# Attention and expert kernel on one core: in the last pair of heads, VectorE instead of GpSimd makes the second halves of the exponentials

## The chip, the cores and the metric

The kernel runs on one core of a Trainium2 chip. A core has five engines that work side by side, each through its own queue in order: TensorE (PE in the profile; PEld is its loading of weights), VectorE (DVE), ScalarE (ACT), GpSimd (POOL) and SyncE (SP), which here only starts transfers (DMA). They wait for one another through semaphores. The metric is the device time of one execution in microseconds (us), median of the runs.

## What is computed

Attention over clusters, and behind it a layer of eight experts of which each token uses two. Cut to what matters:

```python
# q, k, v: (4, 8, 768, 64); 16 centroids per head
mask = q_assign[:, :, :, None] == k_assign[:, :, None, :]
scores = np.where(mask, scale * np.matmul(q, k.transpose(0, 1, 3, 2)), -1e9)
scores = scores - np.max(scores, axis=-1, keepdims=True)
attn = np.exp(scores)
attn = attn / (np.sum(attn, axis=-1, keepdims=True) + 1e-09)
x = np.matmul(attn, v)            # then (3072, 512)
...
# top 2 of 8 experts per token, weights from a softmax of the two
h = np.maximum(x[mask] @ w1[e], 0.0)
out[mask] += top2_w[mask, k, None] * (h @ w2[e])
```

## The kernel before, in words

The 32 heads (4 batches of 8) are worked on as 16 pairs, `p` from 0 to 15. A pair has 12 steps: two heads `s`, and six blocks `kc` of 128 keys each. The loop of `attention` (L262 on) runs over steps `t`, 12 to a pair, and writes the instructions of all engines down in that order; a table `AT` of step numbers says at which step side work is put in. There is no other scheduler: each engine does its instructions in the order in which they are written.

One step of the main loop has three parts:

- `scores` (L477): TensorE makes the scores of 128 keys against 768 queries (four matmuls of 384 columns, L485), and ScalarE their exponentials in two instructions (L486) into a tile `pe` of 128x768 floats, six of which are in use in turn.
- `split_p` (L489), one step later: an exponential is used as the sum of two 16-bit numbers. The first half `hi` costs nothing: it is the upper 16 bits of the float, read in place as bfloat16 with every second element. The second half `lo`, a tile `pl` of 128x768 in float16 (five in turn), is the float minus `hi`, one subtraction (L495). In the kernel before, GpSimd makes all 192 of them.
- `values` (L498), four steps behind the scores: twelve matmuls with `hi` (L512, L514), then six with `lo` (L518), into an accumulator `av` that the two heads share. At the end of a head VectorE divides by the row sums (L523 to L526), and only then can the next head's values begin. At `kc` = 0 no values are made and at `kc` = 1 two rounds of them.

Between these, in the last two pairs (14 and 15), stands side work for the experts:

- GpSimd: the entries of the list of tokens of batch 2 (`g_list`, L697: a tiny memset as a spacer, L700, and an indirect DMA, L701), one per step up to step 183; and in steps 185 to 188 `gather_x` (L923): a tile `xg` is zeroed (L929) and rows of tokens are gathered into it by an indirect DMA (L930). The gathers need the list, which SyncE loads back when all its entries are written (L720).
- ScalarE and VectorE: the weights of the first expert are split into halves (`split_w1`, four pieces of 128x1024; L903 the copy on ScalarE, L904 the subtraction on VectorE).

After the last values come the experts (L731 on). The first instructions of TensorE there are transposes of three gathered tiles (L941), then the logits of the last batch, the gate, and the first expert's layers.

VectorE's largest part, the row maxima of pair p (L457), stands in the steps of the pair before it. In the last pair there is no next pair, and so no maxima.

Of the kernel before, what the change touches and what calls it, by code (L numbers as in the profile page):

```python
# [15 lines left out]
OP = mybir.AluOpType  # L16
# [27 lines left out]
class Kernel:  # L44
# [444 lines left out]
    def split_p(self, p, s, kc):  # L489

        nc, st = self.nc, self.st[p]
        pe = st["p", s, kc].rearrange("p a n -> p (a n)")
        hi = pe.bitcast(BF).rearrange("p (n two) -> p n two", two=2)[:, :, 1]
        lo = self.wk.tile([128, self.S], F16, name="pl", bufs=5)
        nc.gpsimd.tensor_tensor(lo, pe, hi, op=OP.subtract)  # L495
        st["p", s, kc] = hi, lo

    def values(self, p, s, kc):  # L498
# [553 lines left out]
```

## Time and profile before

| what | us |
|---|---|
| median of 3 runs | 1154.22 (1153.69 to 1156.89) |
| the profiled execution | 1154.92 |
| its span | 1153.1 |
| PE busy in the span | 1076.4 (93%) |
| DVE busy | 596.7 (52%) |
| ACT busy | 480.4 (42%) |
| POOL busy | 589.6 (51%) |
| the 192 splits of L495 on POOL | 280.6, 1471 ns each |

How to read it: the shares are means over a program of two halves. Attention takes the first 520 us or so, the experts the rest. Granted clock means the share of TensorE's full clock that it was given (1.00 is 2.4 GHz, 0.50 is 1.2 GHz). An engine that waits is shown with the instruction that released it. All times of the trace are from the start of the span.

### The profile page before, as it was taken

What the parts mean: (1) busy time and instruction counts of PE and PEld (TensorE: products, weight loads), DVE (VectorE), ACT (ScalarE), POOL (GpSimd) and SP (SyncE); (2) the same over time, 40 slices, a digit from 0 to 9 for tenths busy, and PEclk for the clock granted to TensorE, in tenths of its full rate; (3) what the DMA queues carried; (4) which work ended last, traced back from release to release, by engine and by line L of the source; (5) the groups of instructions that cost most, each with busy time, mean ns of one, the idle gap of its engine ahead of it and who ended that gap; (6) DMA issues with size and microseconds to landing.
All of it is one profiled execution on the core that took longest, in us unless ns stands there. A gap on an engine that the chain in (4) does not pass through costs nothing. (4 is left out here: it accounts for less than half of the span.)

```text
span 1153.1 us, 22350 instructions
## 1 busy us (share of the span) xinstructions
PE 1076.4 (93%) x8658; PEld 954.6 (83%) x8658; DVE 596.7 (52%) x1286; ACT 480.4 (42%) x961; POOL 589.6 (51%) x631
## 2 busy tenths in 40 slices
PE   4899899998999899869899999999999999999995
PEld 4588887898888788757799989889898898998984
DVE  5877665876687668436235334433344244433411
ACT  3475656675777566534133303223133132231300
POOL 4776664789578958991645224332343233423311
PEclk8899999999999999969999999999999999999998
DMA  8866776664656444113326225323352244323200
GB/s 224 189 151 152 188 185 194 158 158 110 192 122 159 113 127 122 33 43 118 109 75 210 81 102 166 120 93 109 127 172 73 77 162 129 118 83 131 74 31 31
DMA packets 87678, 144.46 MB, mean 125 GB/s; under 512 B 14296, under 2 KB 65880, under 8 KB 87057
## 3 DMA queue, kind: packets, MB, share of 16 engines
q1 hardware_dynamic: 72272, 106.45, 34.7%
q0 software_dynamic: 13712, 36.42, 9.4%
q8 instruction: 69, 1.13, 0.4%
q10 hardware_dynamic: 1584, 0.13, 0.1%
q14 instruction: 41, 0.33, 0.1%
HBM read 78.21 MB, written 26.53 MB: 91 GB/s over the span
## 5 line engine op out<-in xcount | busy, mean ns | idle before, releaser
L495 POOL TENSOR_TENSOR pl<-pe 128x768 f16<-128x768 f32 x192 | 280.6, 1471 | 97.4 <-ACT pe L486 90.0
L951 PE MATMUL ring<-xT,w1t 128*128 128x416 f32 (+2 forms) x1536 | 290.3, 350 | 0.0
L951 PEld LDWEIGHTS ring<-xT,w1t 128*128 128x128 f32 x1536 | 282.7, 188 | 6.6 <-DVE xT L904 0.3
L990 PE MATMUL ring<-w2t,hT 128*128 128x512 f32 x1152 | 273.7, 394 | 0.0
L990 PEld LDWEIGHTS ring<-w2t,hT 128*128 128x128 f32 x1152 | 214.5, 189 | 43.3
L486 ACT ACTIVATE pe<-ring,l 128x384 f32<-128x384 f32 x384 | 202.9, 578 | 102.5 <-PE ring L485 93.4
L1003 POOL DMA_INDIRECT out<-yo,lst x56 | 65.6, 1172 | 234.7 <-DVE yo L999 187.1
L457 DVE TENSOR_REDUCE aux<-ring 128x1 f32<-128x384 f32 x192 | 107.9, 562 | 94.6 <-PE ring L454 90.2
L485 PE MATMUL ring<-A 128*128 128x384 f32 x384 | 145.4, 379 | 0.0
L485 PE MATMUL ring<-B 128*128 128x384 f32 x384 | 134.3, 350 | 5.0 <-DMA B<-nt 4.9
L960 ACT ACTIVATE hT<-ring 128x416 fp32r<-128x416 f32 (+3 forms) x128 | 56.7, 488 | 180.6 <-PE ring L951 180.5
L961 DVE SCALAR_TENSOR_TENSOR hT<-ring,hT 128x416 fp32r<-128x416 f32 (+3 forms) x128 | 66.2, 553 | 124.0 <-ACT hT L960 123.8
L930 POOL DMA_INDIRECT xg<-xs,lst x56 | 65.5, 1170 | 124.9 <-PE ring L941 105.0
L454 PE MATMUL ring<-A 128*128 128x384 f32 x384 | 114.0, 372 | 14.5 <-DMA A<-mk 8.6
L999 DVE SCALAR_TENSOR_TENSOR yo<-ring,lst,xt 128x512 f32<-128x512 f32 (+1 forms) x49 | 36.7, 750 | 166.6 <-PE ring L990 146.1
L903 ACT ACTIVATE xT<-ring 128x512 fp32r<-128x512 f32 (+1 forms) x56 | 31.0, 565 | 178.0 <-PE ring L941 177.9
L457 DVE TENSOR_REDUCE mm<-ring 128x1 f32<-128x384 f32 x192 | 104.9, 546 | 0.0
L512 PE MATMUL av<-vv,pe 128*128 128x65 f16 x1152 | 100.9, 198 | 0.0
L514 PE MATMUL av<-vv,pe 128*128 128x64 f16 x1152 | 99.9, 196 | 0.0
L454 PEld LDWEIGHTS ring<-A 128*128 128x128 f32 x384 | 71.6, 197 | 31.0 <-ACT pe L486 14.1
L512 PEld LDWEIGHTS <-pe 128*128 128x128 bf16 x1152 | 83.6, 101 | 13.9 <-issue 11.4
L518 PE MATMUL av<-vv,pl 128*128 128x65 f16 x1152 | 68.9, 197 | 20.1 <-POOL spacer L700 12.6
(172 smaller groups left out, 1363.1 us busy)
## 6 DMA issues: line engine op xcount, KB each, us to landing
stg<-in_moe_w SPq DMA_DIRECT2D x64, 512.0 KB
A<-hl SPq DMA_DIRECT2D x30, 384.0 KB
B<-hl SPq DMA_DIRECT2D x30, 384.0 KB
vt<-in_v SPq DMA_DIRECT2D x8, 768.0 KB
out<-zt SPq DMA_DIRECT2D x12, 512.0 KB
xs<-xt SPq DMA_DIRECT2D x4, 1536.0 KB
A<-hl SPq DMA_DIRECT2D x60, 96.0 KB
B<-hl SPq DMA_DIRECT2D x30, 192.0 KB
```

The lines of the kernel that those rows point to most:

```text
L454: nc.tensor.matmul(t, A[:, 0, s, j * 128:j * 128 + 128], A[:, 1, s, n * 384:n * 384 + 384], start=True, stop=True)
L457: nc.vector.tensor_reduce(o, t, axis=X, op=OP.max, negate=True)
L485: nc.tensor.matmul(t, M[:, 1 - qi, s, ks], M[:, qi, s, ns], start=not qi, stop=bool(qi))
L486: nc.scalar.activation(pe[:, n], t, AF.Exp, bias=self.l64[:, 0:1], scale=self.scale)
L495: nc.gpsimd.tensor_tensor(lo, pe, hi, op=OP.subtract)
L512: nc.tensor.matmul(av[:, j, :], ph[:, js], vv[:, hh, kj, 64:129], start=(kc == 0 and j == 0), stop=False, skip_group_check=True)
L514: nc.tensor.matmul(av[:, j, :64], ph[:, js], vv[:, hh, kj, 0:64], start=False, stop=False, skip_group_check=True)
L518: nc.tensor.matmul(av[:, j, :], pl[:, js], vv[:, hh, kj, 64:129], start=False, stop=(kc == NJ - 1), skip_group_check=True)
L951: nc.tensor.matmul(p, self.w1t[:, wi, c, f * 128:f * 128 + 128], self.xT[:, xi, c, n0:n1], start=(i == 0), stop=(i == 3 * ND - 1))
L961: nc.vector.scalar_tensor_tensor(h1, x, 0.0, h0, op0=OP.max, op1=OP.subtract)
L990: nc.tensor.matmul(p, self.hT[:, hi, f, t * 128:t * 128 + 128], self.w2t[:, wi, f], start=(i == 0), stop=(i == 3 * NF - 1))
L1003: i = nc.gpsimd.indirect_dma_start(out=self.out, out_offset=bass.IndirectOffsetOnAxis(ap=en[:r, 0:1], axis=0), in_=yo[:r], in_offset=None, ...
```

## The change

One expression in `split_p`: for the last pair (`p == self.NP - 1`, pair 15) the subtraction is issued to VectorE; for all others to GpSimd as before. An empty line is added too, so every line number behind it is one higher in the kernel after (L495 becomes L496, L904 becomes L905 and so on).

```diff
         lo = self.wk.tile([128, self.S], F16, name="pl", bufs=5)
-        nc.gpsimd.tensor_tensor(lo, pe, hi, op=OP.subtract)
+
+        (nc.vector if p == self.NP - 1 else nc.gpsimd).tensor_tensor(lo, pe, hi, op=OP.subtract)
         st["p", s, kc] = hi, lo
```

The queues of TensorE, ScalarE and SyncE keep their order. VectorE's queue from the end of pair 14 to the end of pair 15, before (`w1t` are the first expert's weights, `rs` the row sums, `xt` the result of attention; each `nt` row is the last step of the row maxima):

```order
L472 TENSOR_TENSOR nt1_8733<-ring_8730,nt0_8732 12x128
L904 TENSOR_TENSOR w1t_8267<-stg_8346,w1t_8267 128x1024
L523 TENSOR_SCALAR rs_8928<-av_8762,am_7126 128x6
L524 RECIPROCAL rs_8928<-rs_8928 128x6
L526 TENSOR_TENSOR xt_7385<-av_8762,rs_8928 128x3x64 x2
L904 TENSOR_TENSOR w1t_8267<-stg_8386,w1t_8267 128x1024
L904 TENSOR_TENSOR w1t_8267<-stg_8426,w1t_8267 128x1024
L904 TENSOR_TENSOR w1t_8267<-stg_8896,w1t_8267 128x1024
L523 TENSOR_SCALAR rs_9134<-av_8962,am_7126 128x6
```

The same place of VectorE's queue after, up to the same row sums:

```order
L496 TENSOR_TENSOR pl_8841<-pe_8801 128x768
L905 TENSOR_TENSOR w1t_8267<-stg_8346,w1t_8267 128x1024
L496 TENSOR_TENSOR pl_8874<-pe_8832 128x768
L496 TENSOR_TENSOR pl_8908<-pe_8865 128x768
L524 TENSOR_SCALAR rs_8928<-av_8762,am_7126 128x6
...
L905 TENSOR_TENSOR w1t_8267<-stg_8386,w1t_8267 128x1024
L496 TENSOR_TENSOR pl_8944<-pe_8899 128x768
L496 TENSOR_TENSOR pl_8960<-pe_8935 128x768
L905 TENSOR_TENSOR w1t_8267<-stg_8426,w1t_8267 128x1024
L496 TENSOR_TENSOR pl_9015<-pe_8951 128x768
L496 TENSOR_TENSOR pl_9049<-pe_9006 128x768
L905 TENSOR_TENSOR w1t_8267<-stg_8896,w1t_8267 128x1024
```

Three splits now stand ahead of pair 14's last row sums, then two behind each of three w1 pieces; the last three stand behind the row sums of pair 15's first head.

GpSimd's queue before, from pair 14's last split (`pl_8810`) on (`tbl` is the list of tokens, `xg` a tile of gathered tokens):

```order
L495 TENSOR_TENSOR pl_8810<-pe_8751 128x768
L700 MEMSET spacer_119 1x1
L701 DMA tbl_116<-rec_7804,pk_7805 32768x2
L495 TENSOR_TENSOR pl_8841<-pe_8801 128x768
...
L701 DMA tbl_116<-rec_7804,pk_7805 32768x2
L495 TENSOR_TENSOR pl_8908<-pe_8865 128x768
L495 TENSOR_TENSOR pl_8944<-pe_8899 128x768
L929 MEMSET xg_8946 128x512
L930 DMA xg_8946<-xs_115,lst0_8268 128x512
L495 TENSOR_TENSOR pl_8960<-pe_8935 128x768
```

And after:

```order
L496 TENSOR_TENSOR pl_8810<-pe_8751 128x768
L701 MEMSET spacer_119 1x1
L702 DMA tbl_116<-rec_7804,pk_7805 32768x2
...
L702 DMA tbl_116<-rec_7804,pk_7805 32768x2
L930 MEMSET xg_8946 128x512
L931 DMA xg_8946<-xs_115,lst0_8268 128x512
L930 MEMSET xg_9001 128x512
L931 DMA xg_9001<-xs_115,lst0_8268 128x512
```

Three list entries and four gathers are left behind pair 14's last split, one straight after the other; the twelve splits of pair 15 are gone from this queue.

## Rows read from the trace of the kernel before

**Rows 1.** Busy time by stretch: length, then each engine, PEclk, DMA

```profile
490.06:520.14 30.08, 20.57 (x248) 17.88 (x248) 9.74 (x11) 10.73 (x18) 28.30 (x28) 0.69 0.15 41
440.00:475.00 35.00, 33.82 (x481) 30.09 (x480) 28.43 (x85) 21.34 (x43) 29.23 (x27) 1.00 0.26 74
500.00:505.00 5.00, 5.00 (x51) 4.38 (x48) 1.67 (x1) 3.27 (x5) 4.61 (x5) 0.50 0.19 53
```

**Rows 2.** Waits from 490 to 521 us: us in total, times, longest

```profile
PEld L518 <- POOL pl L495: 8.3, 7, 2.4
```

**Rows 3.** Timeline of POOL: start us, us, instruction, idle time before it

```profile
481.50 0.98 POOL L701 DMA_INDIRECT tbl<-rec,pk  x1 [0.17 <-issue]
...
484.19 0.99 POOL L701 DMA_INDIRECT tbl<-rec,pk  x1 [0.17 <-issue]
485.19 1.49 POOL L495 TENSOR_TENSOR pl<-pe 128x768 f16<-128x768 f32 x1
...
486.87 1.76 POOL L701 DMA_INDIRECT tbl<-rec,pk  x1 [0.17 <-issue]
...
490.32 0.99 POOL L701 DMA_INDIRECT tbl<-rec,pk  x1 [0.17 <-issue]
491.33 1.49 POOL L495 TENSOR_TENSOR pl<-pe 128x768 f16<-128x768 f32 x1
...
496.46 1.76 POOL L701 DMA_INDIRECT tbl<-rec,pk  x1 [0.18 <-issue]
...
511.15 0.53 POOL L929 MEMSET xg<- 128x512 f32 x1
...
513.01 7.16 POOL L495 TENSOR_TENSOR pl<-pe 128x768 f16<-128x768 f32 x5
...
548.44 1.98 POOL L701 DMA_INDIRECT tbl<-rec,pk  x1 [0.21 <-issue]
```

**Rows 4.** Timeline of DVE, the same columns

```profile
484.91 2.86 DVE L904 TENSOR_TENSOR w1t<-stg,w1t 128x1024 fp32r<-128x1024 f32 x1 [8.82 <-ACT w1t L903]
490.58 0.22 DVE L523 TENSOR_SCALAR rs<-av,am 128x6 f32<-128x6 f32 x1 [2.81 <-PE av L518]
...
491.60 2.30 DVE L904 TENSOR_TENSOR w1t<-stg,w1t 128x1024 fp32r<-128x1024 f32 x1
494.13 3.23 DVE L904 TENSOR_TENSOR w1t<-stg,w1t 128x1024 fp32r<-128x1024 f32 x1 [0.22 <-ACT w1t L903]
503.33 2.22 DVE L904 TENSOR_TENSOR w1t<-stg,w1t 128x1024 fp32r<-128x1024 f32 x1 [5.97 <-ACT w1t L903]
```

**Rows 5.** Groups by shape, DVE: count | busy us, mean ns | idle before

```profile
L904 DVE TENSOR_TENSOR xT<-ring,xT 128x512 fp32r<-128x512 f32 x48 | 32.6, 688 | 17.4 <-ACT xT L903 17.4
```

**Rows 6.** Line L495, whole span: ns min/median/max, first and last start

```profile
L495 POOL TENSOR_TENSOR pl<-pe x192: 1457/1468/1498, 51.9 to 518.7; 128x768 f16<-128x768 f32 x192
```

**Rows 7.** Line L904 up to 600 us, the same columns

```profile
L904 DVE TENSOR_TENSOR w2t<-stg,w2t x4: 1215/1226/1227, 544.3 to 551.1; 128x1024 fp32r<-128x1024 f32 x4
```

**Rows 8.** Timeline of ACT, columns as in rows 3

```profile
485.11 1.05 ACT L486 ACTIVATE pe<-ring,l 128x384 f32<-128x384 f32 x2 [0.23 <-PE ring L485]
```

**Rows 9.** Timeline of PE, columns as in rows 3

```profile
490.19 0.35 PE L518 MATMUL av<-vv,pl 128*128 128x65 f16 x6 [1.94 <-POOL spacer L700]
...
502.22 0.52 PE L518 MATMUL av<-vv,pl 128*128 128x65 f16 x6
...
504.67 0.47 PE L518 MATMUL av<-vv,pl 128*128 128x65 f16 x6
...
520.23 0.51 PE L518 MATMUL av<-vv,pl 128*128 128x65 f16 x6 [0.26 <-POOL pl L495]
520.55 2.21 PE L941 MATMUL ring<-ident,xg 128*128 128x128 f32 x12
```

**Rows 10.** Line L930 from 485 to 520 us; POOLq is GpSimd's sequencer

```profile
L930 POOLq EVENT_SEMAPHORE  x5: 17/17/8055, 493.0 to 508.5; - x5
...
DMA to landing us min/median/max: 3.5/3.5/3.6
```

## The prediction

> **What bounds the kernel now.** I read the page's slices first: over the whole span TensorE is busy 93%, but the slices between about 480 and 520 us, where the last pair of heads is worked on, show it emptier, at a lower clock, and GpSimd full. So I took that stretch apart. Between 490.06 us (the end of pair 14's last split, for which TensorE's row at 490.19 waited [rows 9]) and 520.14 us, GpSimd is busy 28.30 of 30.08 us, TensorE 20.57 at a mean granted clock of 0.69, VectorE 9.74, ScalarE 10.73; from 440 to 475 us TensorE had been busy 33.82 of 35 us at a clock of 1.00 [rows 1]. The list of waits names the reason: the loads of the second halves wait for the GpSimd splits, 8.3 us in seven waits [rows 2]. In this stretch GpSimd runs one queue without a gap: twelve splits with a pitch of 1.43 us (the last five take 7.16 us), three list entries (L701), four gathers with their zeroing [rows 3]. 12 x 1.43 = 17.2 us of the 30.08 are the splits; the other 12.9 are the list entries and gathers between them. The last values of TensorE begin at 520.23, the first transposes of the experts at 520.55 [rows 9]: TensorE goes straight on, so whatever this stretch loses, the end of the program loses.
>
> **The change, part by part.**
>
> *What leaves GpSimd.* The twelve splits, 17.2 us of its queue. What stays (12.9 us) is needed by TensorE only through the gathers, below.
>
> *What a split costs on VectorE.* No row of before shows it. The nearest are the same subtraction on VectorE: 128x1024 with both inputs in SBUF, undisturbed, 1.226 us [rows 7], and 128x512 with one input in PSUM, 0.688 us [rows 5]. Between them lie 512 elements and 0.538 us, 1.05 ns per element, so 768 elements take 0.688 + 256 x 1.05 ns = 0.957 us. A lower end is 768/1024 of the longer one, 0.92; an upper end adds one whole GpSimd split, 1.468 [rows 6], as a blocker: 2.43. That VectorE is held up by a GpSimd split is in the rows: the four w1 subtractions beside splits took 2.86, 2.30, 3.23 and 2.22 us instead of 1.23 [rows 4]. I take 0.957, because in the last 17 us no split is left on GpSimd.
>
> *Where the twelve lie.* Three of them (the first three of pair 15) have their exponentials ready by 486.16 us at the latest (the third one's are the ScalarE row at 485.11, 1.05 us) [rows 8], and VectorE idles 8.82 us before its row at 484.91 [rows 4] and again from 487.77 to 490.58. They are done before 490.5, beside the other work. Nine are left.
>
> *What VectorE must do from there.* Its order is fixed by the program: one group of row sums (490.58 to 491.60, 1.02 us), w1, two splits, w1, two splits, w1, two splits, the next group of row sums, three splits. Two groups 2.04, three w1 subtractions at 1.226 = 3.68 (they took 2.30 + 3.23 + 2.22 = 7.75 beside splits [rows 4]; that goes, too), nine splits 8.61: together 14.33 us.
>
> *What the rest of GpSimd does to it.* Three list entries and four gathers are left beside these 14.33 us. The w2 subtractions, which run beside list entries, take 1.215 to 1.227 us, so the lower end is 0; if each of the seven blocked VectorE for its whole length (about 1 us [rows 3]) it were 7. I take 2.0 for this, nearer to the row, and 0.5 for moments in which an exponential or a buffer isn't ready: 2.5.
>
> *What the early splits do to pair 14.* Up to 490 us GpSimd still makes pair 14's splits, with a list entry between each two, and TensorE waits for them. List entries get longer beside a VectorE subtraction with two SBUF inputs: 0.99 us at 484.19 and 490.32, 1.76 at 486.87, with the subtraction of 484.91 to 487.77 beside it, and 1.98 at 548.44 beside a w2 subtraction [rows 3, 4, 7]. Two more entries of pair 14 (those at 481.50 and 484.19, 0.99 each) will now have a split beside them: 2 x 0.77 = 1.5 us later for TensorE. Bounds: 0, and 3 for four of them.
>
> The Trainium skill differs here (SBUF — State Buffer, Who interferes with whom): it infers that a tensor_tensor takes only the read side of the pair shared with GpSimd, while descriptors need the write side, so that it would not stall them. By that the 1.5 us would be 0 and the sum 1.5 us better; the entries of 1.76 and 1.98 us speak against it, and I keep 1.5.
>
> *The gathers' cover.* TensorE's first transposes need three gathers. Pair 14's last split ends at 490.06 + 1.5 = 491.6. Three list entries at a pitch of 1.27 (490.06 to 491.33) to 2.05 us (1.76 + what lies around it) end at 495.4 to 497.7. The first gather could go 2.83 us after the last entry: that ran from 496.46 to 498.22 [rows 3], and GpSimd's sequencer waited for the loaded list from 493.0 for 8.055 us, to 501.05 [rows 10]. So 498.2 to 500.5; the third gather starts two pitches of 1.86 (511.15 to 513.01 [rows 3]) later, 501.9 to 504.2, and lands 3.5 us on [rows 10]: 505.5 to 507.8. TensorE wants it at about 509 (below), so 1 to 3.5 us of cover are left; if it is gone, TensorE waits for what is missing.
>
> *TensorE as the next limit.* From 500 to 505 us the granted clock is 0.50, the lower of TensorE's two levels (1.2 GHz) [rows 1]. At that level one step, scores and one round of values, takes 504.67 - 502.22 = 2.45 us [rows 9], of which about 1.0 is the values. Eight steps and four more rounds are 8 x 2.45 + 4 x 1.0 = 23.6 us at 1.2 GHz, 11.8 at 2.4. At before's mean clock of 0.69 it would be 17.1, about as long as VectorE's chain (16.8): just covered, and a fuller TensorE has had the higher clock [rows 1].
>
> **The sum.** Pair 14's values ended at 490.19 + 0.35 = 490.54 [rows 9]. 490.54 + 1.5 + 14.33 + 2.5 = 508.9 for the end of the last split, which before was 513.01 + 7.16 = 520.17 [rows 3]: 11.3 us earlier. What follows the last split (values, row sums, transposes) is the same on both sides, and all of it waits for engines, nothing for a clock time, so the 11.3 us reach the end. The profiled execution took 1154.92 us (span 1153.1): 1143.6. It lies 0.7 above the median of the runs, so on that scale 1142.9, rounded 1143. With the lower ends (0 and 0): 504.9, 15.3 us, 1138.9. With the upper ends (3 and 7.5): 515.4, 4.8 us, 1149.4.
>
> **The rivals.**
> *A starting VectorE split holds GpSimd's.* Three splits of pair 14 have a VectorE split beside them; if each were held for 0.957 us, TensorE would lose 2.9 more: 1143 + 2.9 = 1145.9. Against it: all 192 splits took 1457 to 1498 ns [rows 6], also the one at 485.19 that began after the w1 subtraction at 484.91. It is what the Trainium skill states (SBUF — State Buffer, the section on its two separate sides): whichever of the two starts first keeps the shared ports for the whole instruction. The trace has only GpSimd's split winning.
> *The gathers come last.* If the list ends at the late end, 500.5, after a start 1.5 us later still, and three gathers are 0.77 us longer each, the third lands at 500.5 + 1.5 + 3.7 + 2.3 + 3.5 = 511.5, where TensorE wants it at 509.5 (the end of the last split and 0.57 us of values): 2 us, 1145.
> *TensorE stays at 1.2 GHz.* 492.0 + 23.6 = 515.6 for the last values, against 520.74: 5.1 us, 1154.2 - 5.1 = 1149.1. Against: 1.00 where it is busy [rows 1].
> *The operand costs double.* The split reads floats and every second bfloat16; if VectorE needed two cycles per element, 0.957 + 0.81 = 1.76 each: 490.54 + 1.5 + 2.04 + 3.68 + 2.5 + 15.8 = 516.1, 4.1 us, 1150.
> *Slower: the ports.* VectorE is held in every split as it was in the w1 subtractions: nine at 2.43 = 21.9, w1 at 7.75, start 3 later: 490.54 + 3 + 2.04 + 7.75 + 21.9 = 525.2, 5.0 us later, 1159.2. It turns to a loss when a split costs over 1.87 us in that case. For it speak [rows 4]; against it that these were blocked by splits, which are gone.
> *The change gains the stretch and the end doesn't move*: something behind 520 us gives it back, 1154. I find no wait there that doesn't hang on an engine.
>
> **How the numbers follow.** Forecast with its near cases 0.62, GpSimd held 0.08, gathers 0.10, clock 0.06, double price 0.06, slower 0.04, nothing 0.04. A measurement of this kernel tells about 0.3%, 3.5 us, from no change. The first four and half of the double price are faster: 0.89; same 0.07; slower 0.04. The range is that of the bounds, 1139 to 1149.5; it leaves out the last three cases, about 0.14.
>
> **What would show it.** The twelve splits as VectorE rows of about 0.96 us, the first three up to 2.4; the three w1 rows behind them at about 1.23; list entries of 1.4 to 1.8 at 481 to 496; the first transposes of L941 (one line further on) at about 509 without a wait for the gathers; and from there to the end the same 632.5 us as now (1153.1 - 520.55). The prediction falls if a VectorE split takes over 1.3 us when no GpSimd split is beside it, if pair 14's last split ends later than 493, or if that last stretch grows.

## The result and the profile after

| | before | after |
|---|---|---|
| median, us | 1154.06 (1153.69 to 1157.43, 6 runs) | 1144.01 (1139.18 to 1145.87, 6 runs) |
| ratio, 95% interval | | 0.9896 (0.9871 to 0.9920) |
| the profiled execution, us | 1154.92 | 1145.87 |
| its span, us | 1153.1 | 1144.0 |
| PE busy | 1076.4 | 1072.6 |
| DVE busy | 596.7 | 603.8 |
| POOL busy | 589.6 | 571.5 |

The change makes the kernel 10 us faster; the forecast was 1143.

First the stretch of [rows 1] in the changed kernel, and below it the time from the end of pair 14's last values to the last values of pair 15; columns as there (length, busy time of PE, PEld, DVE, ACT, POOL, granted clock, DMA). The last two lines go from the start of pair 14's last values to that of pair 15's, first in the kernel before, then in the changed one:

```profile
490.06:520.14 30.08, 26.40 (x375) 22.47 (x376) 19.79 (x32) 19.19 (x39) 14.29 (x20) 0.89 0.45 143
494.25:510.35 16.10, 15.03 (x243) 13.69 (x243) 13.52 (x20) 10.21 (x18) 10.46 (x15) 0.84 0.25 64
...
490.19:520.23 30.04, 20.58 (x249) 17.88 (x249) 9.74 (x11) 10.73 (x18) 28.30 (x26) 0.69 0.15 40
...
493.74:510.35 16.61, 15.54 (x248) 14.20 (x249) 13.52 (x20) 10.21 (x18) 10.83 (x15) 0.83 0.24 62
```

GpSimd, busy for 28.30 us of these 30.08 before, is now busy for 14.29, and TensorE for 26.40 instead of 20.57. Between pair 14's last values and pair 15's, VectorE is fuller than GpSimd, 13.52 of 16.10 us against 10.46; TensorE is fuller than both, 15.03. The exact length of that stretch is read from TensorE's rows. This is TensorE's timeline (start, length, instruction, idle time before it), to be set against [rows 9]:

```profile
493.74 0.51 PE L519 MATMUL av<-vv,pl 128*128 128x65 f16 x6 [1.66 <-POOL spacer L701]
...
507.08 0.20 PE L513 MATMUL av<-vv,pe 128*128 128x65 f16 x1 [1.07 <-DVE xt L527]
...
510.35 0.35 PE L519 MATMUL av<-vv,pl 128*128 128x65 f16 x6
510.54 0.63 PE L942 MATMUL ring<-ident,xg 128*128 128x128 f32 x4
```

From the start of pair 14's last L519 to that of pair 15's it is 510.35 - 493.74 = 16.61 us; before it was 520.23 - 490.19 = 30.04 [rows 9]. This measure, called **the last pair's stretch** below, serves for all experiments, since it doesn't depend on when the pair starts. It is 13.43 us shorter. TensorE's idle time in it fell from 30.04 - 20.58 = 9.46 us, all of it waits for GpSimd, to 1.07, and its busy time for the same matmuls from 20.58 to 15.54, at a granted clock of 0.83 instead of 0.69: 8.39 us are waits that went, and 5.04 us go with the higher clock, whose cause these runs don't show. Yet the span is only 9.1 shorter. The rest: pair 14's last values begin 3.55 us later (493.74 against 490.19), the transposes stand 0.13 closer to the last values, and from the first transposes to the end it is 1144.0 - 510.54 = 633.46 us against 632.55, 0.91 more. 13.43 + 0.13 - 3.55 - 0.91 = 9.1.

The twelve splits themselves, grouped by engine (count, then ns shortest/median/longest, first and last start), and the w1 subtractions up to 600 us:

```profile
L496 POOL TENSOR_TENSOR pl<-pe x180: 1458/1469/1628, 52.2 to 492.2; 128x768 f16<-128x768 f32 x180
L496 DVE TENSOR_TENSOR pl<-pe x12: 946/951/2222, 485.2 to 508.7; 128x768 f16<-128x768 f32 x12
L905 DVE TENSOR_TENSOR w1t<-stg,w1t x6: 1215/1220/1226, 488.0 to 599.4; 128x1024 fp32r<-128x1024 f32 x6
```

A split takes 0.951 us on VectorE, and only one was long, 2.22. The w1 subtractions, 2.22 to 3.23 before [rows 4], are all back at 1.22 in this execution. VectorE's chain of the last pair, in the same columns as [rows 4]:

```profile
487.95 1.23 DVE L905 TENSOR_TENSOR w1t<-stg,w1t 128x1024 fp32r<-128x1024 f32 x1 [1.79 <-ACT w1t L904]
489.10 3.09 DVE L496 TENSOR_TENSOR pl<-pe 128x768 f16<-128x768 f32 x2
494.29 0.23 DVE L524 TENSOR_SCALAR rs<-av,am 128x6 f32<-128x6 f32 x1 [2.10 <-PE av L519]
...
495.32 1.22 DVE L905 TENSOR_TENSOR w1t<-stg,w1t 128x1024 fp32r<-128x1024 f32 x1
496.45 1.84 DVE L496 TENSOR_TENSOR pl<-pe 128x768 f16<-128x768 f32 x2
498.57 1.23 DVE L905 TENSOR_TENSOR w1t<-stg,w1t 128x1024 fp32r<-128x1024 f32 x1 [0.28 <-ACT w1t L904]
499.71 1.96 DVE L496 TENSOR_TENSOR pl<-pe 128x768 f16<-128x768 f32 x2
503.04 1.23 DVE L905 TENSOR_TENSOR w1t<-stg,w1t 128x1024 fp32r<-128x1024 f32 x1 [1.38 <-ACT w1t L904]
504.19 1.82 DVE L496 TENSOR_TENSOR pl<-pe 128x768 f16<-128x768 f32 x2
505.93 0.22 DVE L524 TENSOR_SCALAR rs<-av,am 128x6 f32<-128x6 f32 x1
506.18 0.19 DVE L525 RECIPROCAL rs<-rs 128x6 f32<-128x6 f32 x1
506.40 0.62 DVE L527 TENSOR_TENSOR xt<-av,rs 128x192 f32<-128x192 f32 x2
506.94 2.71 DVE L496 TENSOR_TENSOR pl<-pe 128x768 f16<-128x768 f32 x3
```

The reader is to see one queue in which the idle times are short (0.28 and 1.38 us, both for a w1 copy on ScalarE), and where it is felt. TensorE's only wait in the stretch is the 1.07 at 507.08, for the row sums of the first head (L527, done at 507.02), and these stand behind two splits. From there TensorE makes its six rounds of values in 510.54 - 507.08 = 3.46 us, so the last three splits are nearly free. What VectorE waited 1.38 us for is this copy, the second row, which stands in ScalarE's queue behind exponentials that had themselves waited for TensorE's scores:

```profile
499.62 1.05 ACT L486 ACTIVATE pe<-ring,l 128x384 f32<-128x384 f32 x2 [1.09 <-PE ring L485]
...
501.95 1.06 ACT L904 ACTIVATE w1t<-stg 128x1024 fp32r<-128x1024 f32 x1
```

So the end is set by TensorE up to about 500 us, then by ScalarE's copy, by VectorE's chain from 503.04 to the row sums, and by TensorE again. Two engines are nearly equally long here.

GpSimd in the meantime, columns as [rows 3]:

```profile
487.86 0.99 POOL L702 DMA_INDIRECT tbl<-rec,pk  x1 [0.18 <-issue]
488.88 1.63 POOL L496 TENSOR_TENSOR pl<-pe 128x768 f16<-128x768 f32 x1
...
490.70 1.48 POOL L702 DMA_INDIRECT tbl<-rec,pk  x1 [0.16 <-issue]
492.20 1.48 POOL L496 TENSOR_TENSOR pl<-pe 128x768 f16<-128x768 f32 x1
...
501.69 1.05 POOL L931 DMA_INDIRECT xg<-xs,lst  x1 [3.76 <-issue]
...
505.97 1.01 POOL L931 DMA_INDIRECT xg<-xs,lst  x1 [0.27 <-POOL xg L930]
```

It makes its last split at 492.20, then waits for the list (3.76 us) and gathers. With the landing of 3.5 us of [rows 10] the third gather is there at 505.97 + 3.5 = 509.5, and the transposes begin at 510.54 without a wait for it: about 1 us of cover.

### The profile page after: what moved, and what is told of

The parts are those of the page before. It is cut to its first block, busy times and chain, and to the rows that moved or that the text cites. A ratio compares the mean times of both kernels' runs of the same rounds, so it can differ in the third digit from the quotient of the medians.

```text
span 1144.0 us, 22354 instructions
## 1 busy us (share of the span) xinstructions
PE 1072.6 (94%) x8658; PEld 950.4 (83%) x8658; DVE 603.8 (53%) x1298; ACT 479.4 (42%) x961; POOL 571.5 (50%) x619
## 5 line engine op out<-in xcount | busy, mean ns | idle before, releaser
L496 POOL TENSOR_TENSOR pl<-pe 128x768 f16<-128x768 f32 x180 | 263.3, 1472 | 99.2 <-ACT pe L486 90.3
L454 PE MATMUL ring<-A 128*128 128x384 f32 x384 | 114.7, 373 | 17.1 <-DMA A<-mk 8.6
L904 ACT ACTIVATE xT<-ring 128x512 fp32r<-128x512 f32 (+1 forms) x56 | 31.0, 566 | 173.1 <-PE ring L942 172.8
L485 PEld LDWEIGHTS ring<-B 128*128 128x128 f32 x384 | 74.7, 195 | 6.7 <-issue 4.4
```

The source lines that it names most:

```text
L454: nc.tensor.matmul(t, A[:, 0, s, j * 128:j * 128 + 128], A[:, 1, s, n * 384:n * 384 + 384], start=True, stop=True)
L485: nc.tensor.matmul(t, M[:, 1 - qi, s, ks], M[:, qi, s, ns], start=not qi, stop=bool(qi))
L496: (nc.vector if p == self.NP - 1 else nc.gpsimd).tensor_tensor(lo, pe, hi, op=OP.subtract)
```

## The experiments

The theory: in the last pair GpSimd's queue set the pace (splits, entries, gathers, one behind the other), and now VectorE's does, with fewer and shorter instructions. The main rivals: TensorE at the lower clock is the limit and the engine of the splits only part of it; one head alone holds all the gain, or the gathers do; or the splits that begin early hold up pair 14. The kernel before and the changed one were run again beside them: the kernel before took 1157.31, 1157.27 and 1158.46 us (medians) in the three groups, each of which was run on one chip.

**The changed kernel again** (e4_again; no edit).

> The changed kernel once more. My theory: the stretch from the last values of pair 14 to the first transposes of the experts takes 16.3 us +- 1 (30.0 in the kernel before), the time lies between 1139 and 1146 us, and where pair 14 ends differs by up to 4 us from execution to execution, for reasons that lie before the change (the granted clock of the first 400 us). Rival, the change itself delays pair 14 through the ports that VectorE and GpSimd share: pair 14's last split ends at 493 us or later again, with list entries of over 1.4 us between 478 and 490 us.

Measured: 1142.5 us (1137.26 to 1145.19), ratio 0.9869 (0.9836 to 0.9902). The last pair's stretch is 489.84 to 505.48, 15.64 us. Pair 14's last values begin at 489.84, earlier than before (490.19), though list entries are held here, too. GpSimd in this execution:

```profile
480.64 1.49 POOL L702 DMA_INDIRECT tbl<-rec,pk  x1 [0.18 <-issue]
...
484.83 1.77 POOL L496 TENSOR_TENSOR pl<-pe 128x768 f16<-128x768 f32 x1
...
486.80 1.48 POOL L702 DMA_INDIRECT tbl<-rec,pk  x1 [0.16 <-issue]
```

Two entries 0.5 us longer and one split 0.3 longer: 1.3 us in all. The kernel before had a hold of this kind too, 0.77 us at its entry of 1.76 [rows 3]. So the 3.55 us by which pair 14 was late in the profiled execution aren't a cost of the change. There the lag of GpSimd's splits behind those of before grows long ahead of VectorE's first split at 485.18: 1.7 us at the 25th split, 3.2 at the 109th, 3.66 from the 145th (about 400 us) on, and 3.55 at the last. It is scatter between executions. Two more executions of the changed kernel (e7_after, e10_after, below) have 492.65 and 489.01. The last pair's stretch in the four, and e8_w1_later for use below (us; the clock is the granted one in the stretch):

| execution | stretch | TensorE busy | clock | TensorE's wait for the row sums |
|---|---|---|---|---|
| profiled | 16.61 | 15.54 | 0.83 | 1.07 |
| e4_again | 15.64 | 14.57 | 0.89 | 1.07 |
| e7_after | 16.11 | 15.03 | 0.85 | 1.08 |
| e10_after | 15.69 | 14.64 | 0.89 | 1.05 |
| e8_w1_later | 13.78 | 13.16 | 1.00 | 0.18 |

In the changed kernel the stretch is TensorE's busy time and one wait of 1.05 to 1.08; what differs between executions is the clock.

**Only the first head's six splits on VectorE** (e1_first_head).

```diff
-        (nc.vector if p == self.NP - 1 else nc.gpsimd).tensor_tensor(lo, pe, hi, op=OP.subtract)
+        (nc.vector if (p, s) == (self.NP - 1, 0) else nc.gpsimd).tensor_tensor(lo, pe, hi, op=OP.subtract)
```

> Only the six splits of pair 15's first head go to VectorE, the second head's six stay on GpSimd. My theory, that GpSimd's queue sets the end of the stretch: three list entries (490.06 + 3 x 1.27 = 493.9), the list is back 2.8 later (496.7), three gathers of 1.86 (502.3), a split 1.43, a gather 1.9, five splits 7.2: the last split ends at about 512.8 in the place of 520.2, 7.4 us earlier, 1146.8. Rival, that the gain came from VectorE's w1 subtractions, which ran beside the first head's splits: the whole gain of the change is here, 1144.

**Only the second head's six** (e2_second_head): the same line with `(p, s) == (self.NP - 1, 1)`.

> Only the six splits of pair 15's second head go to VectorE; the first head's stay on GpSimd between its list entries and gathers. My theory: up to the end of the first head (508 us) nothing changes; then TensorE does two rounds of scores and six of values without a wait, 4.8 us at the full clock, 8.7 at 1.2 GHz: the last values end at 513 to 517 in the place of 520.7, 4 to 8 us earlier, 1147 to 1150. The w1 subtractions stay at 2.2 to 3.2 us. Rival as in the run on the first head alone: nearly nothing is gained here, 1153 or more.

Measured: the first head alone 1149.81 us (1148.68 to 1151.74), ratio 0.9927 (0.9902 to 0.9952), stretch 23.84; the second alone 1146.33 (1143.88 to 1149.72), 0.9906 (0.9872 to 0.9941), stretch 23.03. Against the 30.04 of before they save 6.2 and 7.0 us, together 13.2, and both parts at once save 13.43 (14.4 in e4_again). Neither head holds the gain alone. That the halves add up doesn't by itself show that one queue sets the time: TensorE's idle time in the stretch is 9.46 us before, 7.64 and 5.35 with one half and 1.07 with both, and the rest of each saving is its busy time, at clocks of 0.81 and 0.79. The second head's total time fell by more than its stretch, 11.0 us under the kernel before beside it, where 4 to 8 had been expected; between the two profiled executions it is 1153.1 - 1144.5 = 8.6. What else fell these runs don't show. Why each half has its length shows on the engines. With the first head alone, GpSimd still has the second's:

```profile
493.61 1.69 POOL L702 DMA_INDIRECT tbl<-rec,pk  x1 [0.22 <-issue]
...
498.84 1.78 POOL L931 DMA_INDIRECT xg<-xs,lst  x1 [2.99 <-issue]
...
507.55 7.16 POOL L496 TENSOR_TENSOR pl<-pe 128x768 f16<-128x768 f32 x5
```

The gathers are late, and the last five splits wait behind them, 7.16 us in a row as in [rows 3]. They end at 514.71 instead of the 512.8 expected, because I had the first gather at 496.7. The 1146.8 was counted from 1154.2; against the 1157.31 of the kernel before beside it the saving is 7.5 us, where 7.4 had been expected. With the second head alone VectorE works beside GpSimd's splits and is held as in [rows 4]:

```profile
491.12 2.15 DVE L905 TENSOR_TENSOR w1t<-stg,w1t 128x1024 fp32r<-128x1024 f32 x1
494.32 2.39 DVE L905 TENSOR_TENSOR w1t<-stg,w1t 128x1024 fp32r<-128x1024 f32 x1 [1.06 <-ACT w1t L904]
498.14 3.18 DVE L496 TENSOR_TENSOR pl<-pe 128x768 f16<-128x768 f32 x1 [1.43 <-ACT pe L486]
```

A split of 0.951 us takes 3.18 here. That is above even the upper end of the prediction (2.43); splits of over 2 us were seen only where GpSimd makes splits at the same time.

**Every split of the last pair made twice on VectorE** (e3_twice), into the same tile.

```diff
         (nc.vector if p == self.NP - 1 else nc.gpsimd).tensor_tensor(lo, pe, hi, op=OP.subtract)
+        if p == self.NP - 1:
+            nc.vector.tensor_tensor(lo, pe, hi, op=OP.subtract)
```

> As the changed kernel, but VectorE makes each of the twelve splits twice into the same tile. My theory, that VectorE's chain is now the limit in the last pair: nine more splits of 0.92 us stand behind pair 14's end, 8.3 us, of which its idle 1.7 us take some: 6 to 8 us slower than the changed kernel, about 1150 to 1152. Rival, that TensorE (or its clock) is the limit: under 3 us slower.

Measured: 1149.67 us (1146.98 to 1151.55), ratio 0.9927 (0.9900 to 0.9955), which is 7.2 over e4_again on the same chip; the stretch is 24.05 us, 8.4 longer. Nine doubled splits of 0.96 us are 8.6. VectorE has no idle time from 493.24 to 515.56:

```profile
509.89 0.95 DVE L496 TENSOR_TENSOR pl<-pe 128x768 f16<-128x768 f32 x1
510.87 0.96 DVE L498 TENSOR_TENSOR pl<-pe 128x768 f16<-128x768 f32 x1
511.75 0.95 DVE L496 TENSOR_TENSOR pl<-pe 128x768 f16<-128x768 f32 x1
```

So VectorE's queue in the changed kernel has almost no slack: added work comes out at nearly its whole length. That doesn't show that TensorE has any: it is busy for all but 1.07 us of the stretch in the changed kernel. The rival, that TensorE with its clock is a limit, stands beside the theory and not against it.

**Two of VectorE's w1 subtractions later** (e8_w1_later). The other way round: the third and the fourth w1 subtraction are taken out of the chain and put behind the first transposes (ScalarE's copies stay where they are).

```diff
+        for c in (2, 3):
+            self.late_w1(c)
         for hf in range(2):
...
     def split_w1(self, e, c):
+        if isinstance(e, int) and e == 0 and c >= 2:
+            self.nc.scalar.activation(self.w1t[:, 0, c], self.stg[1, c], AF.Copy)
+            return
         self.halves(self.w1t[:, :, c], self.stg[1, c])
 
+    def late_w1(self, c):
+        self.nc.vector.tensor_tensor(self.w1t[:, 1, c], self.stg[1, c], self.w1t[:, 0, c], op=OP.subtract)
```

> The changed kernel, with the third and fourth w1 subtraction of VectorE (2 x 1.23 us) moved behind the first transposes of the experts, where VectorE idles 4.65 us; ScalarE's copies stay. My theory, that VectorE's chain is the limit in the last pair: pair 14's end to the first transposes falls from about 16 us by 1.5 to 2.5 us, and so does the time. Rival, that TensorE with its clock is as long: under 1 us.

The changed kernel on the same chip (e10_after; no edit):

> The changed kernel as the measure for the two others: 0.985 to 0.992 of the kernel before.

Measured: 1141.32 us (1138.62 to 1146.98), ratio 0.9876 (0.9851 to 0.9901), against 1143.58 (1138.03 to 1145.49), 0.9883 (0.9861 to 0.9906), for the changed kernel. By the times alone the two can't be told apart. The stretch is 13.78 us, where four executions of the changed kernel have 15.64 to 16.61. Of these 1.9 to 2.8 us, only 0.4 to 0.5 are idle time of TensorE (0.62 in all instead of 1.05 to 1.08). The rest is its busy time, 13.16 instead of 14.57 to 15.54, at a clock of 1.00 instead of 0.83 to 0.89 (table above). Why the clock stayed at 1.00 these runs don't show: pair 14's last two waits for GpSimd were 1.32 and 1.66 us, as in the profiled execution, where it fell. So what the move gives by itself is not settled, and the rival of this run isn't excluded. TensorE in this kernel (its transposes are L950):

```profile
500.99 0.20 PE L513 MATMUL av<-vv,pe 128*128 128x65 f16 x1 [0.18 <-DVE xt L527]
504.30 1.07 PE L950 MATMUL ring<-ident,xg 128*128 128x128 f32 x8
506.00 0.66 PE L950 MATMUL ring<-ident,xg 128*128 128x128 f32 x4 [0.62 <-DMA xg<-xs,lst]
```

The wait for the row sums has shrunk from 1.07 to 0.18, and the next limit stands behind it: the third transposes wait 0.62 us for a gather. The cover is used up.

**Pair 14's last five splits on VectorE, too** (e5_earlier). The splits of the changed kernel still wait in GpSimd's queue one stage earlier: in pair 14's last five steps TensorE waits 6.0 us for it in the profiled execution.

```diff
-        (nc.vector if p == self.NP - 1 else nc.gpsimd).tensor_tensor(lo, pe, hi, op=OP.subtract)
+        (nc.vector if (p, s, kc) > (self.NP - 2, 1, 0) else nc.gpsimd).tensor_tensor(lo, pe, hi, op=OP.subtract)
```

> The changed kernel, and in pair 14 the last five splits of the second head are VectorE's, too; GpSimd has only list entries and gathers left from there. My theory: GpSimd's pitch of 2.69 us (a split and a list entry) also set the pace of these five steps, while VectorE idled over 5 us before its first split. Pair 15's scores can't begin before the row maxima are in place (the wait for nt, at 483.5 us in the changed kernel), so the gain is what lies behind it: four steps at 1.4 to 2.4 in the place of 2.7 us and an earlier start of VectorE's chain, 3 to 6 us faster than the changed kernel of this call. Rival, that VectorE's chain is full already and only shifts: within 2 us of it.

The changed kernel on the same chip (e7_after; no edit):

> The changed kernel a third time, as the measure for the run with the earlier splits: 1139 to 1146 us, 0.985 to 0.992 of the kernel before. Its executions spread over 6 us or more, and the slower ones have the lower mean granted clock.

Measured: **1139.12 us (1137.93 to 1140.13), ratio 0.9843 (0.9817 to 0.9869)**; the changed kernel 1143.94 (1142.6 to 1146.81), 0.9892 (0.9867 to 0.9916). The ranges don't overlap: 4.8 us better. With e9_both, below, it is the fastest kernel of the study. From the start of pair 14's first split to the first transposes it took 505.68 - 461.58 = 44.10 us, where the four executions of the changed kernel took 46.07 to 47.51: 2.0 to 3.4 of the 4.8 us lie there, and the rest isn't located. The last pair's stretch is no shorter, 15.56, though the clock was 1.00 in it: VectorE is busy for 14.85 of it and TensorE for 13.09, so here VectorE's queue is the longer. GpSimd has only entries and gathers left, and one entry shows what it meets when VectorE's subtractions stand in a row (GpSimd, then VectorE):

```profile
480.03 3.48 POOL L702 DMA_INDIRECT tbl<-rec,pk  x1 [0.21 <-issue]
...
480.00 2.67 DVE L496 TENSOR_TENSOR pl<-pe 128x768 f16<-128x768 f32 x3
```

Three splits of 0.9 us one behind the other hold an entry of 0.96 for 3.48 us.

**Both moves together** (e9_both: the edits of e5_earlier and e8_w1_later).

> The kernel with pair 14's last five splits on VectorE, too, and the same two w1 subtractions moved behind the transposes. My theory: 1.5 to 2.5 us faster than without that move, 6 to 7 us faster than the changed kernel of this call. Rival: as without the move, 4 to 5 us.

Measured: 1138.86 us (1137.04 to 1143.42), ratio 0.9854 (0.9829 to 0.9879), 4.7 under e10_after. That is the gain of the first move alone; the second adds nothing that can be seen. The profile shows VectorE waiting for exponentials (0.93 and 1.18 us) and a clock of 0.73 from 490 to 495 us, where e8_w1_later has 1.00. Which of these takes the 2 us isn't settled by these runs.

**The kernel before, with its gathers behind all splits** (e6_gathers_last). If the gathers alone held the last five splits, putting them last should bring some of the gain without VectorE.

```diff
         for i in range(self.TA):
-            at(z - 7 + i, self.gather_x, 0, i)
+            at(z + 1 / 3, self.gather_x, 0, i)
```

> The kernel before, with the four gathers moved behind the last split on GpSimd. My theory: the splits end 7.7 us earlier (four times 1.86 to 2.07), at 512.5 us, but the third gather starts only at 517 and lands 3.5 us later, at 520.5, so the first transposes wait for it: within 2.5 us of the kernel before. Rival, that GpSimd's queue alone counts: 7 us faster.

Measured: 1163.22 us (1159.81 to 1166.6), ratio 1.0053 (1.0030 to 1.0076): slower by 6 us, which neither side expected. The last pair's stretch did get shorter, 28.5 us. What went wrong stands on three engines. Nine splits now run in one row on GpSimd, and VectorE, which starts a w1 subtraction in their midst, doesn't get through (VectorE, GpSimd):

```profile
503.72 8.86 DVE L904 TENSOR_TENSOR w1t<-stg,w1t 128x1024 fp32r<-128x1024 f32 x1 [5.96 <-ACT w1t L903]
512.51 0.21 DVE L523 TENSOR_SCALAR rs<-av,am 128x6 f32<-128x6 f32 x1
...
498.65 12.86 POOL L495 TENSOR_TENSOR pl<-pe 128x768 f16<-128x768 f32 x9
```

The subtraction ends at 512.58, about 1 us after the last of the nine (511.51); the row sums queue behind it, TensorE waits 5.3 us for them, and GpSimd 3.50 us for TensorE. Then the gathers, issued from 517.21 on, meet the store `xs<-xt` of 1536 KB (TensorE; landing times of the gathers; last a window of the timeline's end, whose last three numbers are granted clock, DMA share and GB/s):

```profile
520.81 0.66 PE L941 MATMUL ring<-ident,xg 128*128 128x128 f32 x4 [1.34 <-DMA xg<-xs,lst]
522.71 1.11 PE L941 MATMUL ring<-ident,xg 128*128 128x128 f32 x4 [1.24 <-DMA xg<-xs,lst]
529.49 1.12 PE L941 MATMUL ring<-ident,xg 128*128 128x128 f32 x4 [5.67 <-DMA xg<-xs,lst]
...
DMA to landing us min/median/max: 3.6/6.1/8.5
...
520.00:530.00 10.00, 2.28 (x11) 1.64 (x12) 1.99 (x4) 1.19 (x2) 3.40 (x7) 0.62 0.92 329
```

1.34 + 1.24 + 5.67 = 8.25 us of waiting for gathers that landed in 3.5 before [rows 10]; less the 1.5 of the shorter stretch this is about the loss (6.0 us between the medians, 7.9 between the profiled spans). So the place of the gathers in front of the last splits was no fault of the kernel before: it is what covers them.

## Why the prediction was right, step by step

**The bound.** Right for the kernel before: GpSimd's queue set the last pair [rows 1 to 3]; TensorE's 9.46 us of waits in the stretch were all for it, and none are left. Half right for the changed kernel: VectorE's chain has almost no slack (a doubled split costs its length, e3_twice), but TensorE is as good as full beside it, and up to about 500 us it is TensorE that ScalarE and VectorE wait for. Where the clock stayed at 1.00, VectorE's queue was the longer (e5_earlier). That a shortened chain gives back its length isn't shown (e8_w1_later).

**The price of a split.** 0.957 us from two rows of other lengths; measured 0.951. The strided 16-bit operand costs nothing that can be seen, so the double price falls. The three w1 subtractions behind pair 14's row sums fell to 1.22 as said, in e10_after too, where the one ahead of them, beside GpSimd's splits, took 2.85.

**VectorE's chain.** Forecast 14.33 + 2.5 = 16.83 us, from the end of pair 14's values to the end of the last split. Measured 494.25 to 509.65, 15.40. The instructions came out as counted; the term of 2.5 for GpSimd's rest (2.0) and for idle moments (0.5) was too large, it is 15.40 - 14.33 = 1.07, and made up the other way round. Entries and gathers hardly hold VectorE (L905 at 1.22 to 1.23, pairs of splits at 1.82 to 1.96 where 1.82 is undisturbed); the two waits for ScalarE's copies (1.66) are most of it, and neighbouring rows overlap by 0.1 us.

**The early contention.** Forecast 1.5 us on top of the 0.77 that the kernel before loses at its entry of 1.76. Measured: 1.3 us of holds in e4_again; in the profiled execution the entries at 482.49 to 487.86 took 0.99, one split took 1.63 and one entry 1.48, 0.6 us in all. Since the 0.77 of before went, the lag of GpSimd's splits behind those of before grew within pair 14 by 0.5 us in e4_again, 1.0 in e7_after, 0.0 in e10_after and -0.1 in the profiled execution. So the hold is real, but the term was too large. It comes and goes with the moment at which VectorE starts: an entry that begins while a subtraction of VectorE is running is held until it is done (490.70, 1.48, to 492.18; VectorE's split of 2.22 had ended at 491.32); one that had begun before it, or in most cases with it, isn't (485.18, 0.99). By this the trace disagrees with what the Trainium skill infers (SBUF — State Buffer, Who interferes with whom), that a tensor_tensor leaves the issue of descriptors alone. An entry also reads the places to write to, and whether that or the descriptors were held no run here shows.

**GpSimd's splits held by VectorE.** I gave it 0.08. One is held in the profiled execution and one in e4_again, for 0.15 to 0.3 us (1.63 and 1.77) and not for a whole 0.957, because little was left of VectorE's w1 subtraction when the split began: it ended at 489.18 here and at 485.28 in e4_again, and the split 1.32 to 1.33 us after that, where one alone takes 1.47. With that the trace agrees with what the Trainium skill states (SBUF — State Buffer, SBUF: two separate sides), that whoever starts first keeps the shared ports for its whole instruction. The split at 485.19 of the kernel before doesn't fit it: it began 0.28 us after VectorE's subtraction of 484.91 and wasn't held, 1.49 [rows 3, 4]. VectorE is the one that waits longest: its second split of the pair took 2.22 beside the split at 488.88.

**The gathers' cover.** Forecast 1 to 3.5 us, measured about 1: the first gather went 4.3 us after the last entry's end (497.39 to 501.69) instead of 2.83. The rival that they come last was near: e8_w1_later reaches it.

**TensorE's clock.** This step was wrong, and luck covered it. I had TensorE at a mean of 0.69 at 17.1 us, nearly as long as VectorE's chain; the row of before has it busy for 20.57 us at 0.69 [rows 1], longer than the chain. It came out at 15.54 because it was granted 0.83 in the stretch: 0.57 from 495 to 500 us, mostly the 1.2 GHz level, and 1.00, 2.4 GHz, from 500 to 505; TensorE was busy for 5.00 of 5.00 us in both. So a full TensorE doesn't mean the higher clock, as I read [rows 1], whose third row also has it full at 0.50. At 1.00 its work takes 13.16 us (e8_w1_later) and not 11.8. TensorE at the lower level was a limit, beside VectorE's chain: in the four executions the stretch follows its busy time.

**What follows the last split.** Here a step was wrong without harm. I let the end hang on the last split, with the same 0.38 us from there to the transposes (520.17 to 520.55) as before. In the changed kernel it is 0.89 (509.65 to 510.54), because the last three splits are no longer what TensorE waits for: it waits for the row sums (507.02), and behind them makes its six rounds.

**The sum.** Forecast for the end of the last split 508.9, measured 509.65: 2.2 us of later start against 1.4 of shorter chain. That the two misses nearly cancelled is luck. Free of the late start, the change takes 13.4 to 14.4 us out of the last pair's stretch in the four executions, more than the 11.3 forecast; and the 632.5 us behind it came out as 633.46, with 629.8 to 633.0 in other executions of the same kernel. The medians, 10.1 us apart in the first comparison and 13 to 15 in the three groups later, lie on both sides of 11.3.

**The signs of being wrong.** Two of the three that the prediction named came up in the profiled execution: pair 14's last split ended at 493.69, later than 493, and the stretch behind the transposes grew by 0.91 us. Neither is a cost of the change: in e4_again and e10_after the split ended before 490, and the last stretch was 629.8 and 631.3. The third, a VectorE split of over 1.3 us without a GpSimd split beside it, was not seen.

## What to carry to other kernels

Where a loop ends, look which engine has lost its usual work there and which still has all of its own: in the last pair VectorE had no maxima to make and GpSimd had gathers on top. When a wait goes away, look at the engine that had waited: here TensorE was then full, and 5.04 of the 13.43 us were its clock. An instruction that moves to another engine is priced well from the same operation on that engine at two other lengths, but its neighbours count as much: VectorE's split cost 0.95 us alone and 3.18 beside GpSimd's. And once the last stage is relieved, look at the stage before it: the same queue set its pace, too, and five more splits gave 4.8 us.

## What the runs showed of the hardware that was not expected

- VectorE can be shut out for long. A subtraction that came during the fourth of nine GpSimd subtractions in a row took 8.86 us instead of 1.23 and ended 1.07 after the last of them; it got no turn between them (e6_gathers_last). So far the longest hold had been 3.23 [rows 4].
- It goes the other way for GpSimd's indirect transfers: an entry behind three VectorE subtractions in a row took 3.48 us instead of 0.96 (e5_earlier). It ended 0.84 us after the last of them (483.51 against 482.67), and the entry of 1.76 before ended 0.86 after its VectorE subtraction (488.63 against 487.77 [rows 3, 4]): as if it did its work only then. In e9_both it is again 3.48. Elsewhere only the subtraction that was running when an entry began held it (491.32 to 492.18, 0.86 again, though VectorE's next split ran by then); why all three did so here is open.
- A gather lands in 3.5 us on quiet queues and in up to 8.5 beside a store of 1536 KB.
- Executions of one kernel differ by several us before the changed stage is even reached: pair 14's last values began between 489.01 and 493.74 in four executions of the changed kernel. A stretch that starts and ends at the same instructions is freer of this, but not of the clock inside it: 15.64 to 16.61 in these four.
